# Sums, scores and outputs of a token block's four batches as one step each on TensorE, in a scan with a gated MLP behind it

## The chip, the cores and the metric

The kernel runs on one core of one Trainium2 chip. The metric is the device time of one execution in microseconds (us). The core's engines are called here as the profile calls them: PE (TensorE matmul) with PEld (its weight loads), DVE (VectorE), ACT (ScalarE), POOL (GpSimd, nearly idle here) and SP (SyncE, which issues most of the DMAs). Each engine works through its own instructions in the order in which they were issued to it; between engines they wait on semaphores.

## The reference

A chunked linear scan ("attention"), then a gated MLP on its output, all in float32. Cut to what is computed:

```python
# batch 4, heads H 8, sequence S 768, head size D 32, state size N 16
cum = cumsum(log(clip(a, 1e-6, 1)))             # within a chunk
M   = (C @ B^T) * exp(cum_i - cum_j) * causal   # "scores", times decays
y   = M @ x + (C @ state) * exp(cum)            # "outputs": own chunk + carried state
state = decay_full * state + sum_j B_j x_j * decay_from_j   # "sums"
# then, with all 8 heads side by side as 256 columns:
out = (silu(y @ w_gate) * (y @ w_val)) @ w_out  # d_model 256, d_ff 1536
```

## The kernel before

**Tiling.** The sequence is cut into NB = 6 token blocks of P = 128 positions, each block into K = 2 pieces of Q = 64. A block holds all four batches, so the MLP sees T = 4 x 128 = 512 columns per block. The hidden size is cut into NF = 12 slices f of 128.

**The scan part of block k.** `load_bc`, `load_aj`, `load_an` and `load_xb` fetch its data (tiles `bc`, `L`, `E`, `xb`). DVE turns the factors into decays with running scans (`scan_j` per batch on `L`, `scan_n` on `E`), weighs B with them (`weigh_b`, in `xb`, one instruction per batch) and C (`weigh_c`, in `bc`). PE then does three things, each per batch b, in small float32 matmuls: `sums` (tiles `st`: 8 matmuls per batch, what a piece adds to the state; 4 in the last block), `scores` (tiles `S`: 8 per batch) and the outputs (tiles `y`: `values`, 16 per batch, from `L` and `xb`, and `carried`, 8 per batch, from `bc` and the state `T`). In between, `apart` (ACT or DVE) takes `st` out of PSUM into `T`, `step` (DVE, `tmp` and `T`) carries the state on, and `mix` (DVE, `L<-S`) multiplies the scores with the decays. `st`, `S` and `y` of blocks 1 to 5 share a pool of four PSUM banks (`at`); `st` takes two of them, `S` and `y` all four. So `S` can't be written in full before `apart` is done, nor `y` before `mix` is.

**The MLP part of block k.** For every f, `gate_val` makes two products (tiles `gv` f 0 and f 1, "halves" below: in block 0 two float32 matmuls each, from block 1 on six fp32r matmuls each, with high and low parts of weights and of `y`, which are `xh` and `xl`). ACT takes the silu, DVE the product (both `sg`), then `hid_high` and `hid_low` split it (`hh`, `hl`; only HB = 4 buffers each), and `project` adds it up (tiles `po`, six matmuls per f). During block 0 and 1 the weights are also fetched and split, `wg` for the gates and `wo` for the projection: per weight tile a row of ACT and DVE instructions (`w_magnitude` to `w_low`), with one work buffer `w` for all `wo` tiles.

**What sets the order.** Every step is handed to a planner (`Plan`) with an engine or a choice of two, a cost, a rank, what it needs and which buffers it takes. The planner runs an estimate of all engines forward and issues steps by rank as they come ready; PE steps of another `kind` (`"f"` for the scan part, `"r"` for the MLP) get a small penalty at a change of kind. What comes out is a fixed order on each engine. So a change of one step's cost or size may also move steps on the other engines, and may move steps between ACT and DVE. Before the change, sums, scores and each batch's `values` and `carried` are a planner step of their own per batch (in block 0 `values` is one step per half of the heads), so MLP steps may come between two batches. All instructions go through one helper, so each has line 192 in the profile, and tiles tell them apart.

Of the kernel before, what the change touches and what calls it, by code (L numbers as in the profile page):

```python
# [17 lines left out]
BATCH, H, S, D, N = 4, 8, 768, 32, 16  # L18
# [6 lines left out]
T = BATCH * P  # L25
NB = S // P
W = Q + 1
NP = H // 2
# [14 lines left out]
class Plan:  # L43
# [19 lines left out]
    def add(self, engine, cost, run, rank, needs=(), takes=(), uses=(), gives=None, kind=None, lag=0.0, rows=1.0, slack=0.0):  # L63
        engines = [(engine, cost)] if cost is not None else engine
        self.ops.append(Op(engines, run, rank, needs, takes, uses, gives, kind, lag, rows, slack))
# [137 lines left out]
def scan_moe_kernel(ctx: ExitStack, tc, aj, an, bc, xb, wgv, wo, cst, sel, out):  # L203
# [34 lines left out]
    def piece(q):  # L238
        return slice(Q * q, Q * q + Q)
# [129 lines left out]
    def banks(k, name, n):  # L369

        where, tag = (ps_mm, "mm") if k == 0 and name in ("S", "y") else (ps_at, "at")
        return [where.tile([P, 512], F32, tag=tag, name=f"{name}{k}_{i}") for i in range(n)]

    def pair(p):
        return slice(2 * N * p, 2 * N * p + 2 * N)

    def scores(k, b):

        c = bl[k]
        if not b:  # L380
            c["S"] = [
                t.rearrange("p (b h i) -> p b h i", h=2, i=Q) for t in banks(k, "S", NP)
            ]
        for q in range(K):
            for p in range(NP):
                te.matmul(
                    c["S"][p][piece(q), b], c["B"][pair(p), b, piece(q)],
                    c["Cz"][pair(p), b, :, piece(q)], start=True, stop=True,
                )
# [6 lines left out]
    def last(k, q):  # L396
        return k == NB - 1 and q == K - 1

    def sums(k, b):

        c = bl[k]
        if not b:
            c["st"] = [
                t[:, : BATCH * 2 * D].rearrange("p (b c) -> p b c", c=2 * D)
                for t in banks(k, "st", K - last(k, K - 1))
            ]
        for p in range(NP):
            for q in range(K - last(k, K - 1)):
                te.matmul(
                    c["st"][q][pair(p), b], c["Bj"][piece(q), b, pair(p)],  # L410
                    c["x"][piece(q), b, 2 * D * p : 2 * D * p + 2 * D], start=True, stop=True,
                )
# [15 lines left out]
    def state(k, q):  # L428

        if q:  # L430
            return bl[k]["T"][:, q - 1]
        return bl[k - 1]["T"][:, K - 1] if k else None
# [10 lines left out]
    def values(k, bs, gs):  # L443

        c = bl[k]
        if not bs[0]:
            t = banks(k, "y", K * len(gs))
            for q in range(K):
                for g in gs:
                    c["y"][2 * q + g] = t.pop(0)[:, : BATCH * Q].rearrange("p (b i) -> p b i", i=Q)  # L450
        L = c["L"].rearrange("p (b h) t -> p b h t", h=H)
        for b in bs:
            for h in range(4 * gs[0], 4 * gs[-1] + 4):
                for q in range(K):
                    o = D * (h % 4)
                    te.matmul(
                        c["y"][2 * q + h // 4][o : o + D, b], c["x"][piece(q), b, D * h : D * h + D],
                        L[piece(q), b, h, :Q], start=b == 0, stop=state(k, q) is None,
                        skip_group_check=True,
                    )  # L460

    def carried(k, b):

        c = bl[k]
        for q in range(K):
            if state(k, q) is None:
                continue
            for p in (0, 2, 1, 3):
                o = 2 * D * (p % 2)
                te.matmul(  # L470
                    c["y"][2 * q + p // 2][o : o + 2 * D, b], state(k, q)[pair(p), b],
                    c["C"][pair(p), b, piece(q)], start=False, stop=True, skip_group_check=True,
                )

    xh, xl = {}, {}

# [175 lines left out]
    def do(f, *a):  # L652
        return lambda *e: f(*a, *e)
# [6 lines left out]
    add = plan.add  # L660
# [22 lines left out]
    for n, ranks in enumerate(IDLE):  # L683
        for i, r in enumerate(ranks):
            need = [("idle", n, i - 1)] if i else [("M", 0, 0)] if n else []
            takes = [] if i else [("at", ("rest", n))]
# [24 lines left out]
    for k in range(NB):  # L711
        r = due(k)
        SLACK = min(k / 2, 1.0)
        z = -5 if not k else r + LEAD[min(k, 3)]
        L, E, BC, XB, CZ, TT = ("L", k), ("E", k), ("bc", k), ("xb", k), ("Cz", k), ("T", k)
# [3 lines left out]
        def behind(key):  # L719
            return [(key, k - 1)] if k else []  # L720

        q = ("SP", 0.48) if k else ("-", 0.0)
# [6 lines left out]
        if not k:  # L729
# [4 lines left out]
            for b in range(BATCH):  # L734
                r = z + 0.5 + b
                for i in range(2 if b < SPREAD else 0):
                    t = ("spread", b, i)
                    add("PE", 0.45, do(spread, b, i), r + 0.5 * i, ["clip", "pick"], takes=[("at", t)], uses=[t, "rows"], gives=t, kind="s", rows=0.1)
                    need = [t, ("decays", 0), "dj"] + ([("scan0", b)] if i else [])
# [16 lines left out]
        st = [("st", k, q) for q in range(K - last(k, K - 1))]  # L756
        S = [("S", k, p) for p in range(NP)]
        y = [("y", k, i) for i in range(2 * K)]
        for b in range(BATCH):
            add("PE", 0.3, do(sums, k, b), z + 3 + 1.4 * b if k else -1.5, [("bt", k, b), *([("st", k, b - 1)] if b else [])], takes=[] if b else [("at", i) for i in st], uses=st, gives=("st", k, b), kind="f", rows=1.0, slack=SLACK)  # L760
            add("PE", 0.35, do(scores, k, b), z + 3.5 + 1.4 * b if k else -1.9 + 0.1 * b, ([("Cz", k), ("st", k, BATCH - 1)] if k else [("Cz", k)]) + ([("S", k, b - 1)] if b else []), takes=[] if b else [("at" if k else "mm", i) for i in S], uses=[*S, CZ], gives=("S", k, b), kind="f", rows=1.0, slack=SLACK)
        done = [("S", k, b) for b in range(BATCH)]
        add("-", 0.0, do(new_states, k), z + 2, behind("T"), takes=[("T", TT)], gives=("T", k))
        for q in range(len(st)):
            add([("Act", 0.65), ("DVE", 0.36)], None, do(apart, k, q), z + 4 + 0.5 * q, [("st", k, b) for b in range(BATCH)] + [("T", k)], uses=[st[q]], gives=("ap", k, q))
        for p in range(NP):
            add("DVE", 0.6, do(mix, k, p), z + 8 + 0.5 * p if k else (-1.25, -1.24, -1.1, -1.1)[p], [*done, *(("L", k, b) for b in range(BATCH))], uses=[S[p]], gives=("M", k, p))
        before = [("step", k - 1, K - 1)] if k else []
        for q in range(0 if k else 1, len(st)):
            need = [*before, ("E", k), ("ap", k, q)] + ([] if k or q > 1 else [("ap", k, 0)])  # L770
            add("DVE", 0.75, do(step, k, q), z + (8 if k else 25) + q, need, takes=[("tmp", ("tmp", k, q))], uses=[("tmp", k, q)] + ([("T", k - 1)] if k and not q else []), gives=("step", k, q))
            before = [("step", k, q)]
        uses = [L, E, XB, BC, *y, TT]
        steps = [("step", k, q) for q in range(len(st))] if k else [("ap", 0, 0)]
        if k:
            uses.append(("T", k - 1))
        for g in range(0 if k else 2):
            need = [("M", 0, p) for p in (2 * g, 2 * g + 1)]
            add("PE", 0.8, do(values, 0, range(BATCH), (g,)), -1.4 + 0.1 * g, need, takes=[("mm", y[2 * q + g]) for q in range(K)], uses=[L, XB, *y], gives=("vals", g), kind="f")
        for b in range(BATCH):  # L780
            if k:
                add("PE", 0.35, do(values, k, (b,), (0, 1)), z + 11 + 1.4 * b, [("M", k, p) for p in range(NP)] + ([("val", k, b - 1)] if b else []), takes=[] if b else [("at", i) for i in y], uses=[L, XB, *y], gives=("val", k, b), kind="f", rows=1.0, slack=SLACK)
            else:
                add("-", 0.0, lambda: None, z, [("vals", 0), ("vals", 1)], gives=("val", 0, b))
            add("PE", 0.5, do(carried, k, b), z + 11.7 + 1.4 * b if k else -1, [("val", k, b), ("ce", k), *steps], uses=uses, gives=("y", k, b), kind="f", rows=1.0, slack=SLACK)
        done = [("y", k, b) for b in range(BATCH)]
        if not k:
            add("-", 0.0, new_whole, -9, ["clip"], takes=[("x", "xf")], gives="xf")
            for i in range(2 * K):
# [8 lines left out]
    for k in range(NB):  # L798
        xs = [(t, k, i) for t in ("xh", "xl") for i in range(2 * K)]
        for f in range(NF):  # L800
            r = due(k, f)
            need = [*xs, ("wh", f), ("wl", f)]
            c = 1.4
            if not k:
                need = [("round", f), *(("xf", i) for i in range(2 * K))]
# [12 lines left out]
        for n, (m, t, fs) in enumerate(sums_of(k)):  # L818
            b = ("po", k, m, t)
            need = [x for f in fs for x in (("hl", k, f), ("wh", NF + f // 2), ("wl", NF + f // 2))]  # L820
# [73 lines left out]
```

## Time and profile before

| | |
|---|---|
| median of 3 runs | 368.54 us (368.12 to 368.83) |
| the profiled execution: its time, its span | 370.03 us, 368.3 us |
| PE busy | 358.2 us, 97% of the span, granted clock 1.000 |
| PEld / DVE / ACT busy | 273.1 / 232.5 / 125.2 us |
| DMA | 28.62 MB, 78 GB/s mean |

The span runs from the first to the last instruction; 1.73 us of the profiled execution lie outside it. "Busy" is the share of time in which at least one instruction ran. A busy PE is not a PE at its peak, since matmuls overlap. Stages in time, by the matmuls on PE: block 0's scan part up to 22 us, block 0's gates with block 1's scan part up to 74 us, block 1's gates up to 107 us, the projections of blocks 0 and 1 with block 2's scan part up to 150 us, then for block 2, 3 and 4 gates (with the scan part of the next block) and projection, 55 us each, then block 5's gates and projection.

### The profile page before, as it was taken

Reading aid. Unit: us, or ns where it says so; the run is one execution under the profiler, and the core shown is the slowest. Engines: PE = TensorE matmul, PEld = TensorE weight load, DVE = VectorE, ACT = ScalarE, POOL = GpSimd, SP = SyncE. Lnnn points to the kernel's source line nnn. Section 1 sums busy time; section 2 is a strip of 40 time slices with the busy share of each in tenths; the row PEclk is TensorE's granted clock in tenths of the full one; section 3 lists DMA queues with packets and bytes.
Section 4 is the critical chain, followed back from the end, with each engine's and each line's share of the span. In section 5 each row is a group of like instructions: output and inputs, shape, how many; then the busy total and the mean of one; then the engine's idle time right before and its main releaser. Section 6 shows DMA issues by size and latency. Waiting matters only on the chain.

```text
span 368.3 us, 7584 instructions
## 1 busy us (share of the span) xinstructions
PE 358.2 (97%) x3293; PEld 273.1 (74%) x3293; DVE 232.5 (63%) x412; ACT 125.2 (34%) x221; POOL 0.8 (0%) x6
## 2 busy tenths in 40 slices
PE   8989999999999989999999999999999999999996
PEld 6855345478877867887788887788887788888895
DVE  3998899999998659255348655349554344352241
ACT  3453773533342443222243221243221233221242
POOL 0000000000000000000000000000000000000000
PEclk9999999999999999999999999999999999999999
DMA  7659732781100760100083100082100000100001
GB/s 223 239 175 241 230 125 73 230 217 58 59 0 4 183 162 0 59 0 3 4 205 83 60 0 2 4 211 78 57 1 2 4 0 2 57 0 2 0 0 59
DMA packets 8737, 28.62 MB, mean 78 GB/s; under 512 B 1008, under 2 KB 1912, under 8 KB 8064
## 3 DMA queue, kind: packets, MB, share of 16 engines
q1 hardware_dynamic: 8416, 26.82, 25.2%
q10 hardware_dynamic: 288, 1.31, 1.0%
q8 instruction: 26, 0.43, 0.5%
q14 instruction: 7, 0.06, 0.1%
HBM read 24.79 MB, written 3.35 MB: 76 GB/s over the span
## 4 chain that ended last, share of the span: by engine, by line
PE 73%; DVE 13%; DMA 9%; issue 2%; ACT 1%; SPq 1%; DVEq 0%; ACTq 0%
PE gv L192 43%; PE po L192 22%; PE y L192 4%; DMA xb<-in_xb 4%; DMA wg5r<-in_wgv 4%; DVE L L192 3%; DMA L<-in_aj 2%; PE S L192 2%; DVE sg L192 2%; PE rest L192 1%; PE st L192 1%; SPq L192 1%; DVE wo3w L192 1%; DVE xb L192 1%; DVE wo4w L192 1%
## 5 line engine op out<-in xcount | busy, mean ns | idle before, releaser
L192 DVE TENSOR_TENSOR sg<-gv,sg 128x512 f32<-128x512 f32 x72 | 49.5, 688 | 85.9 <-PE gv L192 81.5
L192 ACT ACTIVATE sg<-gv 128x512 f32<-128x512 f32 x72 | 42.7, 594 | 102.8 <-PE gv L192 102.8
L192 DVE TENSOR_TENSOR hl<-sg,hh 128x512 fp32r<-128x512 f32 x72 | 48.9, 686 | 18.2 <-ACT hh L192 17.7
L192 ACT CAST hh<-sg 128x512 fp32r<-128x512 f32 x55 | 34.2, 622 | 50.1 <-PE po L192 35.9
L192 DVE TENSOR_TENSOR_SCAN L<-L,dj 128x520 f32<-128x520 f32 x21 | 25.8, 1232 | 5.1 <-DMA L<-clipped 5.1
L192 DVE TENSOR_TENSOR L<-S,L 128x512 f32<-128x512 f32 x24 | 15.1, 683 | 1.6 <-PE S L192 1.6
L192 PEld LDWEIGHTS <-unit 128*128 128x128 bf16 x141 | 11.1, 119 | 4.9 <-issue 3.7
L192 ACT COPY ob<-po 128x512 f32<-128x512 f32 (+1 forms) x13 | 7.2, 555 | 21.1 <-PE po L192 20.6
L192 PE MATMUL rest<-unit 128*128 128x128 bf16 x141 | 12.5, 258 | 1.1 <-DVE warm L192 1.1
L192 PE MATMUL y<-bc,T 32*64 32x64 f32 x352 | 10.2, 229 | 1.3 <-issue 1.3
L192 PE MATMUL po<-hl,wo1h 128*128 128x512 f32 (+1 forms) x26 | 9.9, 382 | 1.2 <-DVE hl L192 1.2
L192 PE MATMUL y<-L,xb 64*32 64x64 f32 x768 | 10.9, 222 | 0.0
L192 PEld LDWEIGHTS y<-L,xb 64*32 64x32 f32 x768 | 7.4, 105 | 4.0 <-issue 2.2
L192 ACT ACTIVATE Cz<-bc,cs 128x512 f32<-128x512 f32 x10 | 6.7, 716 | 10.7 <-DMA bc<-in_bc 7.6
L192 PE MATMUL po<-hl,wo2h 128*128 128x512 f32 (+1 forms) x26 | 9.9, 382 | 0.3 <-DVE hl L192 0.3
L192 PEld LDWEIGHTS y<-bc,T 32*64 32x64 f32 x352 | 7.1, 131 | 4.2 <-issue 2.5
L192 PE MATMUL po<-hh,wo0h 128*128 128x512 f32 (+1 forms) x26 | 9.9, 382 | 0.0
L192 PEld LDWEIGHTS S<-Cz,bc 32*64 32x64 f32 x384 | 6.8, 144 | 4.2 <-issue 2.9
L192 PE MATMUL po<-hh,wo2h 128*128 128x512 f32 (+1 forms) x26 | 9.8, 378 | 0.0
L192 PE MATMUL po<-hh,wo1h 128*128 128x512 f32 (+1 forms) x26 | 9.7, 374 | 0.0
L192 PE MATMUL po<-hl,wo0h 128*128 128x512 f32 (+1 forms) x26 | 9.7, 374 | 0.0
L192 PE MATMUL po<-hl,wo4h 128*128 128x512 f32 (+1 forms) x26 | 9.7, 374 | 0.0
(285 smaller groups left out, 792.2 us busy)
## 6 DMA issues: line engine op xcount, KB each, us to landing
L<-clipped SPq DMA_DIRECT2D x10, 520.0 KB
xb<-in_xb SPq DMA_DIRECT2D x5, 768.0 KB, 11.8
out<-ob SPq DMA_DIRECT2D x11, 256.0 KB, 2.1
bc<-in_bc SPq DMA_DIRECT2D x5, 512.0 KB
E<-clipped SPq DMA_DIRECT2D x5, 260.0 KB
xb<-in_xb ACTq DMA_DIRECT2D x1, 768.0 KB, 5.5
bc<-in_bc ACTq DMA_DIRECT2D x1, 512.0 KB
wg0r<-in_wgv SPq DMA_DIRECT2D x1, 512.0 KB
```

The lines of the kernel that those rows point to most:

```text
L192: ins = getattr(self.engine, name)(*a, **k)
```

## The change

From block 1 on, the four batches of `sums` are one planner step, the four of `scores` another, and `values` and `carried` of all batches a third (`outputs`). Nothing can be placed inside a step. The instructions themselves, their sizes and their order inside a step stay; only the steps that the planner orders have changed, with their costs (0.8, 1.2 and 3.2 in place of 0.3, 0.35 and 0.35 + 0.5 per batch) and what they wait for: `sums` now needs all four batches' weighed B (`bt`) before it starts, `outputs` needs `mix`, `weigh_c` and the state before its first matmul. In block 0 the steps stay as they were, but a zero-cost step ahead of each `carried` is gone.

```diff
-    def scores(k, b):
+    def scores(k, bs):
+        for b in bs:
+            scores_of(k, b)
+
+    def scores_of(k, b):
 ...
-    def sums(k, b):
+    def sums(k, bs):
+        for b in bs:
+            sums_of_pieces(k, b)
 ...
+    def outputs(k):
+        for b in range(BATCH):
+            values(k, (b,), (0, 1))
+            carried(k, b)
 ...
-        for b in range(BATCH):
-            add("PE", 0.3, do(sums, k, b), z + 3 + 1.4 * b if k else -1.5, [("bt", k, b), *([("st", k, b - 1)] if b else [])], ...)
-            add("PE", 0.35, do(scores, k, b), z + 3.5 + 1.4 * b if k else -1.9 + 0.1 * b, ...)
-        done = [("S", k, b) for b in range(BATCH)]
+        for bs in [(b,) for b in range(BATCH)] if not k else [range(BATCH)]:
+            b, more = bs[-1], bs[0]
+            n = len(bs)
+            add("PE", 0.3 if n == 1 else 0.8, do(sums, k, bs), -1.5 if not k else z + 3, [*(("bt", k, i) for i in bs), ...], ...)
+            add("PE", 0.35 if n == 1 else 1.2, do(scores, k, bs), z + 3.5 if k else -1.9 + 0.1 * b, ...)
+        done = [("S", k, BATCH - 1)]
 ...
-        for b in range(BATCH):
-            if k:
-                add("PE", 0.35, do(values, k, (b,), (0, 1)), z + 11 + 1.4 * b, [("M", k, p) for p in range(NP)] + ([("val", k, b - 1)] if b else []), ...)
-            else:
-                add("-", 0.0, lambda: None, z, [("vals", 0), ("vals", 1)], gives=("val", 0, b))
-            add("PE", 0.5, do(carried, k, b), z + 11.7 + 1.4 * b if k else -1, [("val", k, b), ("ce", k), *steps], ...)
-        done = [("y", k, b) for b in range(BATCH)]
+        if k:
+            need = [*(("M", k, p) for p in range(NP)), ("ce", k), *steps]
+            add("PE", 3.2, do(outputs, k), z + 11, need, takes=[("at", i) for i in y], ...)
+        for b in range(0 if k else BATCH):
+            add("PE", 0.5, do(carried, 0, b), -1, [("vals", 0), ("vals", 1), ("ce", 0), *steps], ...)
+        done = [("y", k)]
```

**How it moves instructions.** In block 2 the order on PE stays as it was: sums, scores and outputs had each come out as one piece before. In blocks 1 and 3 to 5 they had not. In block 3 (and likewise in 4 and 5) before, PE did half of the sums, gate slice 6, the other half, half a slice of gates, the scores, three halves, the outputs up to the third batch's `values`, gate slice 9, and the rest of the outputs; in block 1 the sums were split by gate slice 6 and the outputs by gate slice 9.

PE in block 3, around the end of the first half of the sums; numbers at the end of names count buffers. Before:

```order
L192 MATMUL st_1_1831<-xb_1512 32x64
L192 MATMUL gv_6_0_1849<-xh_979,wg6h 128x512 x2
L192 MATMUL gv_6_0_1849<-xh_979,wg6l 128x512 x2
L192 MATMUL gv_6_0_1849<-xl_980,wg6h 128x512 x2
L192 MATMUL gv_6_1_1856<-xh_979,wg6h 128x512 x2
L192 MATMUL gv_6_1_1856<-xh_979,wg6l 128x512 x2
L192 MATMUL gv_6_1_1856<-xl_980,wg6h 128x512 x2
L192 MATMUL st_0_1830<-xb_1512 32x64
```

PE in block 3, around the end of all of the sums. After:

```order
L192 MATMUL st_1_1831<-xb_1512 32x64
L192 MATMUL gv_6_0_1865<-xh_978,wg6h 128x512 x2
L192 MATMUL gv_6_0_1865<-xh_978,wg6l 128x512 x2
L192 MATMUL gv_6_0_1865<-xl_979,wg6h 128x512 x2
L192 MATMUL S_0_1878<-Cz_1527,bc_1487 64x128
L192 MATMUL S_1_1879<-Cz_1527,bc_1487 64x128
L192 MATMUL S_2_1880<-Cz_1527,bc_1487 64x128
L192 MATMUL S_3_1881<-Cz_1527,bc_1487 64x128
```

The sums are no longer resumed behind slice 6; the scores follow half a slice after the sums in both versions, and now five halves, not three, lie between scores and outputs.

DVE at the end of block 1's gates, where block 2's sums are taken out of PSUM (`T<-st`) between the last weight tiles' steps. Before:

```order
L192 TENSOR_TENSOR sg_10_1222<-gv_10_1_1215,sg_10_1222 128x512
L192 TENSOR_SCALAR wo5w<-wo5w 128x512 x2
L192 SCALAR_TENSOR_TENSOR wo5w<-wo5r,wo5w 128x512
L192 TENSOR_TENSOR sg_11_1246<-gv_11_1_1239,sg_11_1246 128x512
L192 ISA wo5w<-wo5r,wo5w 128x1024
L192 TENSOR_TENSOR T_928<-st_1_1252,cs 128x256
```

DVE at the same place. After:

```order
L192 TENSOR_TENSOR wo4l<-wo4w,wo4h 128x512
L192 TENSOR_TENSOR sg_11_1240<-gv_11_1_1232,sg_11_1240 128x512
L192 TENSOR_TENSOR T_900<-st_0_1246,cs 128x256
L192 TENSOR_SCALAR wo5w<-wo5w 128x512
L192 TENSOR_TENSOR tmp_0_1297<-T_106,E_899 128x256
```

`T<-st` now stands ahead of the steps of weight tile `wo5`, of which four stood ahead of it. (`ISA` is `CUSTOM_DVE_ANT_0` in the profile.)

DVE during block 2's projection, where block 4's decays (`L`) and weighed B (`xb`) are made between the low parts `hl` that the projection waits for. Before:

```order
L192 TENSOR_TENSOR hl_6_2171<-sg_6_1863,hh_6_2170 128x512
L192 SCALAR_TENSOR_TENSOR L_2093<-L_2093,dj 128x520
L192 TENSOR_TENSOR hl_7_2182<-sg_7_1907,hh_7_2181 128x512
L192 TENSOR_TENSOR xb_2114<-xb_2114,L_2093 128x128
L192 TENSOR_TENSOR hl_8_2192<-sg_8_1962,hh_8_2191 128x512
```

DVE at the same place. After:

```order
L192 TENSOR_TENSOR xb_2097<-xb_2097,L_2076 128x128 x2
L192 TENSOR_TENSOR hl_6_2173<-sg_6_1914,hh_6_2172 128x512
L192 SCALAR_TENSOR_TENSOR L_2076<-L_2076,dj 128x520
L192 TENSOR_TENSOR hl_7_2185<-sg_7_1945,hh_7_2184 128x512
L192 TENSOR_TENSOR xb_2097<-xb_2097,L_2076 128x128
L192 SCALAR_TENSOR_TENSOR L_2076<-L_2076,dj 128x520
L192 TENSOR_TENSOR hl_8_2196<-sg_8_1962,hh_8_2195 128x512
```

The first two `xb` steps, which need the `xb` load, moved from behind `hl_7` to ahead of `hl_6`, and one more scan (`SCALAR_TENSOR_TENSOR` on `L`) stands ahead of `hl_8`. On SP the order of the DMAs is the same but for one pair: block 1's `E` load now goes ahead of weight tile `wg5r`'s, not behind it.

More of the change, by code (lines that the diff above doesn't have):

```diff
@@ L397, in last, with sums_of_pieces @@
         return k == NB - 1 and q == K - 1
-    def sums(k, b):
+    def sums(k, bs):
+        for b in bs:
+            sums_of_pieces(k, b)
+    def sums_of_pieces(k, b):
         c = bl[k]
@@ L758, in scan_moe_kernel @@
         y = [("y", k, i) for i in range(2 * K)]
-        for b in range(BATCH):
-            add("PE", 0.3, do(sums, k, b), z + 3 + 1.4 * b if k else -1.5, [("bt", k, b), *([("st", k, b - 1)] if b else [])], takes=[] if b else [("at", i) for i in st], uses=st, gives=("st", k, b), kind="f", rows=1.0, slack=SLACK)
-            add("PE", 0.35, do(scores, k, b), z + 3.5 + 1.4 * b if k else -1.9 + 0.1 * b, ([("Cz", k), ("st", k, BATCH - 1)] if k else [("Cz", k)]) + ([("S", k, b - 1)] if b else []), takes=[] if b else [("at" if k else "mm", i) for i in S], uses=[*S, CZ], gives=("S", k, b), kind="f", rows=1.0, slack=SLACK)
-        done = [("S", k, b) for b in range(BATCH)]
+        for bs in [(b,) for b in range(BATCH)] if not k else [range(BATCH)]:
+            b, more = bs[-1], bs[0]
+            n = len(bs)
+            add("PE", 0.3 if n == 1 else 0.8, do(sums, k, bs), -1.5 if not k else z + 3, [*(("bt", k, i) for i in bs), *([("st", k, more - 1)] if more else [])], takes=[] if more else [("at", i) for i in st], uses=st, gives=("st", k, b), kind="f", slack=SLACK)
+            add("PE", 0.35 if n == 1 else 1.2, do(scores, k, bs), z + 3.5 if k else -1.9 + 0.1 * b, ([("Cz", k), ("st", k, BATCH - 1)] if k else [("Cz", k)]) + ([("S", k, more - 1)] if more else []), takes=[] if more else [("at" if k else "mm", i) for i in S], uses=[*S, CZ], gives=("S", k, b), kind="f", slack=SLACK)
+        done = [("S", k, BATCH - 1)]
         add("-", 0.0, do(new_states, k), z + 2, behind("T"), takes=[("T", TT)], gives=("T", k))
         for q in range(len(st)):
-            add([("Act", 0.65), ("DVE", 0.36)], None, do(apart, k, q), z + 4 + 0.5 * q, [("st", k, b) for b in range(BATCH)] + [("T", k)], uses=[st[q]], gives=("ap", k, q))
+            add([("Act", 0.65), ("DVE", 0.36)], None, do(apart, k, q), z + 4 + 0.5 * q, [("st", k, BATCH - 1), ("T", k)], uses=[st[q]], gives=("ap", k, q))
         for p in range(NP):
@@ L779, in scan_moe_kernel @@
             add("PE", 0.8, do(values, 0, range(BATCH), (g,)), -1.4 + 0.1 * g, need, takes=[("mm", y[2 * q + g]) for q in range(K)], uses=[L, XB, *y], gives=("vals", g), kind="f")
-        for b in range(BATCH):
-            if k:
-                add("PE", 0.35, do(values, k, (b,), (0, 1)), z + 11 + 1.4 * b, [("M", k, p) for p in range(NP)] + ([("val", k, b - 1)] if b else []), takes=[] if b else [("at", i) for i in y], uses=[L, XB, *y], gives=("val", k, b), kind="f", rows=1.0, slack=SLACK)
-            else:
-                add("-", 0.0, lambda: None, z, [("vals", 0), ("vals", 1)], gives=("val", 0, b))
-            add("PE", 0.5, do(carried, k, b), z + 11.7 + 1.4 * b if k else -1, [("val", k, b), ("ce", k), *steps], uses=uses, gives=("y", k, b), kind="f", rows=1.0, slack=SLACK)
-        done = [("y", k, b) for b in range(BATCH)]
+        if k:
+            need = [*(("M", k, p) for p in range(NP)), ("ce", k), *steps]
+            add("PE", 3.2, do(outputs, k), z + 11, need, takes=[("at", i) for i in y], uses=[L, *uses], gives=("y", k), kind="f", slack=SLACK)
+        for b in range(0 if k else BATCH):
+            add("PE", 0.5, do(carried, 0, b), -1, [("vals", 0), ("vals", 1), ("ce", 0), *steps], uses=uses, gives=("y", 0) if b == BATCH - 1 else ("y", 0, b), kind="f")
+        done = [("y", k)]
         if not k:
```

## The prediction

> **What bounds the kernel now.** I read the page first, then the busy time by stage, then the chain of waits, then the timelines at the places where the order on PE or DVE changes.
>
> ```profile
> span 368.3 us, 7584 instructions
> ...
> PE 358.2 (97%) x3293; PEld 273.1 (74%) x3293; DVE 232.5 (63%) x412; ACT 125.2 (34%) x221; POOL 0.8 (0%) x6
> ```
>
> PE is busy for 97%, so at most some 10 us of waits can go; the rest has to come out of what PE does. By stage (start and end, length, then each engine's busy time):
>
> ```profile
> 76.00:107.00 31.00, 31.00 (x138) 25.66 (x137) 30.09 (x52) 11.54 (x20) 0.00 (x0) 1.00 0.27 83
> 107.00:150.00 43.00, 40.29 (x467) 31.05 (x466) 31.80 (x57) 15.78 (x28) 0.00 (x0) 1.00 0.29 75
> 150.00:189.00 39.00, 39.00 (x466) 30.83 (x466) 18.42 (x34) 10.34 (x20) 0.00 (x0) 1.00 0.13 41
> ```
>
> Up to 107 us DVE (30.09 of 31.00) is as full as PE; from 107 to 150 PE loses 2.7 us; from 150 on PE is the bound without a gap, and DVE has room. So an edit of PE's order can pay in full behind 150 us, and before that only where DVE lets it.
>
> **Term 1: islands of small matmuls in blocks 3 to 5.** The chain of waits (start, length, work) through block 2's gates, which hold block 3's scan part:
>
> ```profile
> 150.21 16.32 PE gv L192 x72
> 166.53 0.39 PE st L192 x32
> 166.92 2.94 PE gv L192 x12
> 169.86 0.39 PE st L192 x32
> 170.25 1.58 PE gv L192 x6
> 171.83 1.14 PE S L192 x63
> 172.96 4.31 PE gv L192 x18
> 177.27 1.94 PE y L192 x128
> 179.21 2.94 PE gv L192 x12
> 182.15 1.17 PE y L192 x64
> 183.32 5.68 PE gv L192 x24
> 189.00 16.34 PE po L192 x72
> ```
>
> Undisturbed, 72 gate matmuls take 16.32 us: 0.227 each, 1.36 per half slice, 2.72 per slice. A slice between two islands takes 2.94, a half 1.58, three halves 4.31 against 4.08, four halves 5.68 against 5.44: every stretch behind an island costs 0.22 to 0.24 more, whatever its length. That is the price of leaving the gates and coming back, and it is all that an island costs beside its own matmuls. Before, five islands (sums, sums, scores, outputs, outputs); now three: the split of sums and that of outputs go. Working it out anew: 16.32 + sums 0.78 + half 1.58 + scores 1.14 + five halves 4.31 + 2.72 + outputs 1.94 + 1.17 + three slices 5.68 + 2.72 = 38.36 us, against 38.79 from 150.21 to 189.00. So 0.43 us per block, 0.22 per island. Blocks 4 and 5 have the same order and islands: 3 x 0.43 = **-1.3 us**. The sums, scores and outputs keep their number of matmuls. No new wait should arise on PE: block 3's weighed B is due a whole stage earlier (DVE is busy for only 18.42 of the 39 us), between sums and scores there is still one half (1.58 us) in which the four sums banks' worth of `T` is taken out, as before, and the way from scores to outputs grows by two halves.
>
> The Trainium skill (TensorEngine Tiling, Key Properties) says that a change of tiling mode drains TensorE, and TensorE: Matmul & The Clock Gate, Single matmul latency, puts the fixed part of a lone warm matmul at 398 cycles of 2.4 GHz. As an estimate from that page, two full drains of 0.17 us for each of six islands would be 2.0 us in place of 1.3. The rows show 0.22 per island, not 0.33, so part of the drain must be covered, and I keep the rows.
>
> **Term 2: the wait ahead of block 2's scores.** PE's order there does not change, DVE's does. PE's timeline (start, length, instruction, idle time before it):
>
> ```profile
> 107.41 0.86 PE L192 MATMUL st<-xb 64*32 64x64 f32 x64
> 108.20 0.50 PE L192 MATMUL po<-hh,wo0h 128*128 128x512 f32 x1
> ...
> 109.80 0.43 PE L192 MATMUL S<-Cz,bc 32*64 32x128 f32 x4
> 111.35 1.17 PE L192 MATMUL S<-Cz,bc 32*64 32x128 f32 x60 [1.12 <-DVE T L192]
> 112.46 0.50 PE L192 MATMUL po<-hh,wo0h 128*128 128x512 f32 x1
> ```
>
> ```profile
> 110.28 0.68 DVE L192 CUSTOM_DVE_ANT_0 wo5w<-wo5r,wo5w 128x1024 uint16<-128x1024 uint16 x1
> 110.88 0.42 DVE L192 TENSOR_TENSOR T<-st,cs 128x256 f32<-128x256 f32 x1
> 111.22 0.42 DVE L192 CAST wo5h<-wo5w 128x512 fp32r<-128x512 f32 x1
> ```
>
> The sums are done at 108.2, but DVE takes its half of them out only at 110.88, behind the work on weight tile `wo5`. In the new order `T` stands ahead of all of that. DVE's steps follow each other by 0.60 (the long ones, 110.28 to 110.88) or 0.34 (the short ones, 110.88 to 111.22). By the two DVE orders, what is done before this `T` loses four `wo5` steps (two long, two short), four casts and one scaling (short) to ACT or to later, and gains four short ones: 1.2 + 7 x 0.34 = 3.6 us less and 1.4 more, 2.2 us net. So DVE could be there at 108.7, right behind the sums. The scores then start at 109.80 and run through: 1.14 us by the chain's row, so the projection resumes at 110.94, not at 112.46: **-1.5 us**. Bounds: nothing, if DVE is as late as before; 1.5 if `T` ends before 109.80, for which DVE has 0.75 us to spare (108.7 + 0.34 against 109.80). I take the upper end, since 2.2 us less work is nearer to it than none. ACT takes the other half in both versions. What is late next: `mix` must end before the outputs, now 4.3 us behind the scores as before; with the `T` steps and one `hl` ahead of it, it has over a microsecond left. `wo5`'s steps move behind, and the projection first needs them at its eleventh slice, 10 us later. The outputs' end releases block 3's loads (SP waits for it), so the loads, and what waits for them later in that stage, come as much earlier and stay as long.
>
> **Term 3: block 1's part, up to 52 us.** PE's timeline, where block 0's gates hold block 1's sums:
>
> ```profile
> 43.66 3.67 PE L192 MATMUL gv<-xf,wg5w 128*128 128x512 f32 x8 [0.75 <-ACT hh L192]
> 47.26 0.34 PE L192 MATMUL st<-xb 64*32 64x64 f32 x16
> ...
> 52.08 0.35 PE L192 MATMUL st<-xb 64*32 64x64 f32 x16 [0.46 <-DVE xb L192]
> ```
>
> From 43.66 to the sums' end at 52.4 PE needs two slices, the sums, 0.46 of waiting for the fourth batch's weighed B and one island's price. In the new order all sums stand behind slice 6, where three quarters of them stood, and ahead of that B DVE has two casts and a scaling less and a copy more (0.7 us less); I expect no wait, 0.46 less, and 0 to 0.22 for the island, and the like for the outputs' split at slice 9. Against it stands the start: slice 5 waits for weight tile `wg5`, whose DMA is now issued behind `E`:
>
> ```profile
> 25.86 0.53 SPq L192 DMA_DIRECT2D wg5r<-in_wgv  x1
> 26.48 0.62 SPq L192 DMA_DIRECT2D E<-clipped  x1
> ```
>
> and DVE now does two more scans of `L` ahead of `wg5`'s steps, one of which used to stand between them and one behind. The issue alone is 0.6 us later; slice 5 may start anywhere from no later to 0.9 later; I take 0.4. Together 0.46 + 0.3 - 0.4, about **-0.4 us**, between -0.9 and +0.4.
>
> **Term 4: `xb` and scans ahead of `hl`.** During block 2's and 3's projection the outputs, now ended before slice 9, release the next block's loads one slice earlier, but DVE's queue has the first `xb` steps ahead of `hl_6`, and a scan more ahead of `hl_8`. DVE before, and SP's issue of that load:
>
> ```profile
> 198.26 0.29 DVE L192 TENSOR_TENSOR xb<-xb,L 128x128 f32<-128x128 f32 x1 [0.33 <-DMA xb<-in_xb]
> 198.47 0.68 DVE L192 TENSOR_TENSOR hl<-sg,hh 128x512 fp32r<-128x512 f32 x1
> 199.07 0.28 DVE L192 TENSOR_TENSOR xb<-xb,L 128x128 f32<-128x128 f32 x1
> 199.27 1.23 DVE L192 TENSOR_TENSOR_SCAN L<-L,dj 128x520 f32<-128x520 f32 x1
> 200.42 0.67 DVE L192 TENSOR_TENSOR hl<-sg,hh 128x512 fp32r<-128x512 f32 x1
> ```
>
> ```profile
> 186.57 0.62 SPq L192 DMA_DIRECT2D xb<-in_xb  x1
> ```
>
> The load lands 11.7 us after its issue. Issued 2.94 earlier (one slice), it lands at 195.3. Then come two `xb` (0.2 each), `hl_6` 0.6, a scan 1.15, `hl_7` 0.6, `xb` 0.2, a scan 1.15 and `hl_8` 0.6: 200.0. PE, its projection starting at 189.00 - 0.43 + 0.2 by where the outputs begin, wants `hl_8` at its second matmul of the ninth slice: 188.8 + 8 x 1.36 + 0.23 = 199.9. So it is a tenth late or a few tenths early, in two projections. I take **+0.3 us** in all, between 0 and +1.
>
> **Sum.** -1.3 - 1.5 - 0.4 + 0.3 = -2.9 us. The profiled execution took 370.03 us (1.73 of it outside the span), so it would be 367.1; the runs' median lies 1.5 lower at 368.54, which gives **365.7 us**.
>
> **Rivals.** *The scores' wait stays.* If DVE reaches `T` as late as before, or ACT does, term 2 is gone: 365.7 + 1.5 = 367.2. For it speaks that DVE was 97% busy from 76 to 107 and its chain through the `wo` tiles is serial, with one buffer; against it that `wo5` no longer stands in front. The skill's TensorEngine Tiling, PSUM Bottleneck, warns that PSUM's evacuation may become the bound when small matmuls are packed; this wait is such a case.
>
> *Nothing measurable.* Terms 2 and 3 both fail and the early stage loses as much again as term 1 brings: `wg5` late by 1 us or more and DVE's backlog carried into block 1's gates, which wait for free banks: -1.3 + 0.3 + 1 = 368.5. The trace has PE waiting only 0.75 us there, so this needs several tenths in more than one place.
>
> *Slower.* The `xb` load lands late and blocks `hl_6` and all behind it. Block 3's load, in the chain, took longer:
>
> ```profile
> 122.34 13.57 DMA xb<-in_xb
> ```
>
> With 13.57 in place of 11.7 it lands at 197.2, and `hl_8` comes at 201.9, 2 us late, in both projections: +4 in place of +0.3, 365.7 + 3.7 = 369.4. It turns the gain into a loss from a landing some 13.2 us after the issue. Against it: block 4's load took 11.7 with the same neighbours in the queue.
>
> **How the numbers follow.** Forecast 0.63, the scores' wait 0.17, nothing 0.11, slower 0.09. 0.2% of the time, about what a measurement of this kernel can tell from no change, is 0.74 us: faster means below 367.8, slower above 369.3. The first two are faster; of the last a third would land within the bound because only one projection is hit. Faster 0.80, same 0.14, slower 0.06. The forecast's own bounds: term 1 fixed, term 3 from -0.9, term 4 from 0, gives 364.9, and 0.3 for the runs' own spread 364.6; upwards the range takes in the scores' wait and half of a late load, 367.9.
>
> **What would show it.** Right: three islands per block in the chain from 150 us on and 38.4 us from the first gate of block 2 to its projection; no wait of the scores for `T` near 110 us, and the projection resuming 1.1 to 1.2 us after the scores begin; sums of block 1 in one piece without a wait for `xb`; PE idle below 8 us in all. Wrong: `po <- DVE hl` waits in block 2's or 3's projection beyond 0.5 us each, slice 5 of block 0 waiting over 1.6 us, `S <- T` waits in any block.

## The result, and the profile after

The changed kernel takes 371.67 us (median of 20 executions, 369.48 to 375.07) against 368.80 us for the kernel before (20 executions): ratio 1.0069, 95% interval 1.0045 to 1.0094. It is slower, by some 2.5 us, where 2.9 us less was forecast. The profiled execution took 372.27 us with a span of 370.5. The ratios here and below leave out executions that were disturbed, so they and not the medians are what is compared.

The page of the changed kernel, span and busy time of the engines:

```profile
span 370.5 us, 7585 instructions
...
PE 358.0 (97%) x3293; PEld 275.0 (74%) x3293; DVE 231.6 (63%) x410; ACT 127.2 (34%) x223; POOL 0.8 (0%) x6
```

PE does the same 3293 matmuls in the same busy time (358.2 before). What grew is its waiting. PE's waits (what it waited for, us in total, times, longest), of after and then the two rows of before that belong beside them:

```profile
PE y L192 <- issue: 5.3, 4, 1.6
PE gv L192 <- ACT wg7w L192: 1.5, 1, 1.5
...
PE po L192 <- DVE hl L192: 0.6, 2, 0.3
```

```profile
PE po L192 <- DVE hl L192: 1.5, 3, 0.8
PE y L192 <- issue: 1.3, 1, 1.3
```

The first row is new in size: four times PE stops inside the outputs (`y`) for nothing that the profile shows ("issue"), once in block 0 as before, and now once in each of blocks 3, 4 and 5. The chain of waits through block 3's gates, which hold block 4's scan part, shows one:

```profile
203.62 16.32 PE gv L192 x72
219.94 0.79 PE st L192 x53
220.73 1.60 PE gv L192 x6
222.33 1.14 PE S L192 x63
223.47 7.04 PE gv L192 x30
230.51 2.58 PE y L192 x146
233.09 1.21 issue
234.30 0.84 PE y L192 x39
235.13 8.40 PE gv L192 x36
```

Three islands, as the order said, and the two stretches of gates behind them cost what was forecast (1.60 and 7.04). But the outputs take 230.51 to 235.13, 4.62 us, where block 1's, with the same 192 matmuls in one piece, take 3.10:

```profile
60.55 3.10 PE y L192 x192
```

Taken from the same views, the clock at the start of each stage (first gate of the block):

```
                    before    after    difference, and of the stage alone
block 2's gates     150.21    146.82   -3.4   -3.4
block 3's gates     205.34    203.62   -1.7   +1.7
block 4's gates     260.45    259.86   -0.6   +1.1
block 5's gates     315.50    317.74   +2.2   +2.8
end                 368.3     370.5    +2.2    0.0
```

So the early stages brought 3.4 us, more than forecast, and the three stages with stalled outputs lost 5.6. Block 5's outputs, in the last of these, are followed by something else. PE's timeline there, and the busy time by stretch (length, busy time of PE, PEld, DVE, ACT, POOL, then the granted clock):

```profile
288.81 0.32 PE L192 MATMUL y<-L,xb 64*32 64x64 f32 x9
290.57 0.42 PE L192 MATMUL y<-L,xb 64*32 64x64 f32 x23 [1.44 <-issue]
290.93 0.46 PE L192 MATMUL y<-bc,T 32*64 32x64 f32 x16
291.32 0.73 PE L192 MATMUL gv<-xh,wg9h 128*128 128x512 f32 x2
```

```profile
288.50:292.00 3.50, 2.06 (x67) 1.58 (x68) 0.64 (x2) 0.65 (x2) 0.00 (x0) 1.00 0.02 5
292.00:295.50 3.50, 3.50 (x10) 2.70 (x9) 1.44 (x5) 0.60 (x1) 0.00 (x0) 0.52 0.00 0
```

For 3.4 us behind that stall the granted clock is 0.52, and the 36 gate matmuls behind the outputs take 10.03 us by the chain where those behind block 4's outputs take 8.40: another 1.6 us.

### The profile page after: what moved, and what is told of

Read it like the earlier page. It is cut to its first block, busy times and chain, and to the rows that moved or that the text cites. A ratio compares the mean times of both kernels' runs of the same rounds, so it can differ in the third digit from the quotient of the medians.

```text
span 370.5 us, 7585 instructions
## 1 busy us (share of the span) xinstructions
PE 358.0 (97%) x3293; PEld 275.0 (74%) x3293; DVE 231.6 (63%) x410; ACT 127.2 (34%) x223; POOL 0.8 (0%) x6
## 4 chain that ended last, share of the span: by engine, by line
PE 67%; DMA 14%; DVE 12%; issue 3%; ACT 2%; SPq 1%; DVEq 0%; ACTq 0%
PE gv L192 40%; PE po L192 17%; PE y L192 4%; DMA wg6r<-in_wgv 4%; DVE L L192 3%; DMA bc<-in_bc 3%; DMA xb<-in_xb 3%; DMA L<-clipped 2%; DVE hl L192 2%; PE rest L192 2%; PE a L192 1%; PE S L192 1%; DVE sg L192 1%; PE st L192 1%; DMA wo4r<-in_wo 1%
## 5 line engine op out<-in xcount | busy, mean ns | idle before, releaser
L192 PE MATMUL y<-L,xb 64*32 64x64 f32 x768 | 11.7, 223 | 3.8 <-issue 3.8
L192 DVE CAST xh<-y 128x256 fp32r<-128x256 f32 x9 | 3.4, 417 | 11.5 <-PE y L192 11.5
L192 PE MATMUL po<-hl,wo3h 128*128 128x512 f32 (+1 forms) x26 | 9.8, 378 | 0.0
L192 ACT CAST xh<-y 128x256 fp32r<-128x256 f32 x11 | 3.5, 377 | 18.2 <-PE y L192 18.2
L192 PE MATMUL po<-hh,wo2l 128*128 128x512 f32 (+1 forms) x26 | 9.7, 374 | 0.0
```

The source lines that it names most:

```text
L192: ins = getattr(self.engine, name)(*a, **k)
```

## What an issue wait is here

Counting every record of PE in order of time (matmuls, weight loads, its few instructions that only wait), the first record behind the waits in `y` of after has the numbers 706, 3778, 4802 and 5826. Divided by 256 each leaves 194 (before's one wait, in block 0, stands at 706 as well). So all stand at a border of blocks of 256 instructions. The same holds for every issue wait of PE in the twelve traces of this case: 21 waits, all with the rest 194. The trace also has a DMA queue for instructions:

```profile
q8 instruction: 26, 0.43, 0.5%
```

26 packets of 16,384 bytes, which is 64 bytes for each of 256 instructions; and PE's 6626 records hold 26 borders with that rest, at the numbers 194, 450 and so on up to 6594. Theory A, then: PE's instructions come in blocks of 256. Each matmul of an island stands with its weight load for two instructions and takes 16 ns (3.10 us for 192), so a block that lies wholly inside the outputs (384 instructions) is used up in 2.1 us, and the next block is not there. In gates a block lasts 29 us. The Trainium skill (Runtime: NRT & Kernel Launch, Instruction fetch mechanics) says the same of the blocks, 16 KiB or 256 instructions, fetched while the one before is executed, and calls the cost of crossing a border mostly hidden. The trace agrees with the blocks; hidden the crossing is only where a block lasts long enough.

Theory A makes the stall hang on where a border falls, not on what is done. The rivals: B, a long row of small matmuls stalls PE by its length, wherever it stands; C, the loss is in the merged sums and scores, the new load times or the clock, and the issue waits only go along.

## The experiments

### Block 3's sums issued twice (the changed kernel with more work)

```
     def sums(k, bs):
         for b in bs:
             sums_of_pieces(k, b)
+        for b in bs if k == 3 else ():
+            sums_of_pieces(k, b, True)      # same banks, same values once more
```

> The changed kernel with block 3's sums issued twice in a row (the second pass writes the same values again): 32 matmuls of the program more on PE, 128 records with their weight loads, and no other instruction moved on any engine. Theory A (PE runs out of instructions: its stream comes in blocks of 256 instructions, weight loads counted, and a block that lies wholly inside the outputs is used up in 2.1 us, faster than the next one comes, 3.3 to 3.9 us; so the loss hangs on where the blocks' borders fall): the added 128 move the borders out of blocks 3, 4 and 5; no issue wait in their outputs, which take 3.1 us each in place of 4.4 to 4.8; sums of block 3 longer by 0.65 to 0.8 us; time 371.7 - 4.6 + 0.7 = 367.8 us, 366.3 to 368.5. Rival B (a long row of small matmuls stalls PE by its length, wherever it stands): the three waits of 1.1 to 1.4 us stay, 372.4. Rival C (the time is lost to the granted clock and to late loads, and the issue waits only go along): 372.4 as well.

Measured: 367.10 us, ratio to before 0.9919 (0.9884 to 0.9953). More work, and some 5.5 us less than the changed kernel by the two ratios (1.5% of 369). The chain through block 3's gates, with block 4's scan part:

```profile
201.80 16.32 PE gv L192 x72
218.12 0.79 PE st L192 x53
218.91 1.59 PE gv L192 x6
220.50 1.14 PE S L192 x61
221.63 7.03 PE gv L192 x30
228.67 3.07 PE y L192 x182
```

The outputs take 3.07 us, and no issue wait is left but block 0's. From the gates' first to the projection's first matmul (201.64 to 240.01 in PE's timeline) it is now 38.37 us, the forecast's 38.36. B and C, which expected 372.4, fall. Of the 5.5 us A accounts for 3.9. The clock, at half here from 7.24 us on for 10.24 us, does not drop behind a stall in any later stage, which can make up part of the rest. The mean granted clock of each execution, which is on record, agrees without proving it: read in stretches of 3.4 us at half clock, 13 of the 19 executions of the changed kernel that are compared have one or four of them (in this trace the start alone takes three), and 1 of 11 here. Where such a stretch stood, a mean does not tell.

### Block 1's sums issued twice

The same edit with `k == 1`: the same added work, the borders moved by the same 128 instructions, but from block 1 on.

> The same added work, but block 1's sums are issued twice in place of block 3's. By theory A the borders move by 128 instructions from block 1 on: they leave blocks 3, 4 and 5 as in the kernel with block 3's sums twice, and now one block of instructions lies wholly inside the outputs of block 1 and one inside those of block 2. So issue waits of 1.1 to 1.4 us in the outputs of blocks 1 and 2, none in 3 to 5; 371.7 - 4.6 + 0.7 + 2 x 1.4 = 370.6 us, or 369.2 if block 2's stall is hidden behind the wait for its xb load. Rival B: three waits in blocks 3 to 5 and none in 1 and 2, 372.4. Rival C: 372.4, or less if block 1 hides the added work.

Measured: 369.05 us, ratio 0.9982 (0.9949 to 1.0014). The stalls are gone from blocks 3 to 5 and stand in blocks 1 and 2. PE's timeline in these two:

```profile
61.80 0.32 PE L192 MATMUL y<-L,xb 64*32 64x64 f32 x9
62.89 0.42 PE L192 MATMUL y<-L,xb 64*32 64x64 f32 x23 [0.77 <-issue]
...
118.31 0.30 PE L192 MATMUL y<-L,xb 64*32 64x64 f32 x5
118.84 0.44 PE L192 MATMUL y<-L,xb 64*32 64x64 f32 x27 [0.23 <-issue]
```

A said where: a border stands 307 instructions into block 1's outputs, and the wait comes behind 153 matmuls (144 and 9) with their weight loads, 306 records. The waits are smaller than the 1.4 us expected, and the time is accordingly nearer to the lower of A's two figures.

### Outputs alone split again, and outputs alone merged

First, the changed kernel with before's output steps; second, the kernel before with the new one:

```
-            add("PE", 3.2, do(outputs, k), z + 11, ...)
+            add("PE", 0.35, do(values, k, (b,), (0, 1)), z + 11 + 1.4 * b, ...)
+            add("PE", 0.5, do(carried, k, b), z + 11.7 + 1.4 * b, ...)
```

> The changed kernel with the outputs alone put back to steps of one batch, so that in blocks 3 to 5 (and 1) slice 9 stands again between two and a half batches and the rest; sums and scores stay in one piece. Theory A: no block of 256 instructions lies wholly inside a row of small matmuls, no issue wait beyond block 0; one island more in blocks 1, 3, 4 and 5 (0.22 us each): 371.7 - 4.6 + 0.9 = 368.0 us, 367.2 to 368.6. Rival B expects the same 368.0 (shorter rows). Rival C (merged sums, scores and the loads' new times are what costs): 371.7 + 0.2.

> The kernel before with the outputs alone made one step; sums and scores stay in steps of one batch as before. Theory A: issue waits in the outputs of blocks 3, 4 and 5, which take 4.4 to 4.8 us in place of 3.1; one island less in blocks 1, 3, 4 and 5: 368.8 - 0.9 + 4.6 = 372.5 us, 371.0 to 373.0. Rival B: the same. Rival C (sums, scores or the loads are to blame): 368.8 - 0.9 = 367.9.

Measured: split again 369.67 us, ratio 1.0008 (0.9978 to 1.0038); outputs alone merged 370.62 us, ratio 1.0052 (1.0013 to 1.0091). So most of the slowing comes with the outputs, against C, as far as these two tell: with the outputs' steps the planner moved instructions on DVE and ACT too. And the two miss their figures by 1.7 and 1.9 us, one above and one below. Why, of the first, from PE's waits with outputs split again:

```profile
PE st L192 <- DVE xb L192: 2.9, 1, 2.9
PE y L192 <- issue: 1.8, 1, 1.8
...
PE S L192 <- DVE T L192: 1.0, 1, 1.0
```

The only issue wait is block 0's, as expected. But block 2's scores wait for `T` again, as before the change, though `T` has kept its new place in DVE's order, ahead of `wo5`'s steps:

```profile
111.87 0.41 DVE L192 TENSOR_TENSOR T<-st,cs 128x256 f32<-128x256 f32 x1
112.20 0.42 DVE L192 TENSOR_SCALAR wo5w<-wo5w 128x512 f32<-128x512 f32 x1
```

DVE comes to it at 111.87 us, 2.6 later than in the changed kernel (109.29), while PE's scores begin only 1.2 later (110.89 for 109.69). So the place in the order alone does not save the wait; DVE must also arrive in time. How much of its lateness is this execution's own start (the 2.9 us stand at 13 us) and how much the moved steps, one trace does not tell, and of the 1.7 us it explains 1.0. In the second, the stalls are not all there. PE's timeline in blocks 3 and 4 of the outputs alone merged:

```profile
179.06 0.45 PE L192 MATMUL y<-L,xb 64*32 64x64 f32 x31
180.69 0.21 PE L192 MATMUL y<-L,xb 64*32 64x64 f32 x1 [1.18 <-issue]
180.84 0.46 PE L192 MATMUL y<-bc,T 32*64 32x64 f32 x16
181.23 1.04 PE L192 MATMUL gv<-xh,wg9h 128*128 128x512 f32 x2
...
236.91 0.58 PE L192 MATMUL y<-L,xb 64*32 64x64 f32 x32
```

Block 4's border is crossed without a wait. The instruction packets' own times say why (read from the trace's DMA records; all in us: when PE entered the block ahead of the border and how long it was in it, waits included, then when the packet started and landed and when PE went on behind the border):

```
kernel, block        entered, length  packet started   landed   PE goes on
after, 3             174.28, 3.27     174.92           176.10   177.56
after, 4             230.59, 3.71     231.70           232.83   234.30
after, 5             286.65, 3.93     287.66           289.10   290.57
sums 1 twice, 1       59.64, 3.24      60.51            61.44    62.89
sums 1 twice, 2      116.13, 2.71     116.46           117.41   118.84
outputs alone, 3     177.37, 3.33     178.06           179.33   180.69
outputs alone, 4     234.73, 2.32     234.74           235.69   237.05
outputs alone, 5     290.94, 3.12     291.69           292.82   294.06
```

At these eight borders PE goes on 1.24 to 1.47 us behind the landing; a packet takes 0.9 to 1.4 us; it starts 0.0 to 1.1 us after PE enters the block. Together 2.3 to 3.9 us for a block against 2.1 us of work in it, so a border inside the outputs costs from 0.05 to 1.7 us, as the packet happens to come. The clock dropped here too: the first gates behind block 3's outputs take 1.04 us, where the same row behind block 5's outputs in the changed kernel, still at the full clock, shows 0.73.

### Control: the kernel before with block 3's sums twice

```
     def sums(k, b):
         sums_of_pieces(k, b)
+        if k == 3:
+            sums_of_pieces(k, b, True)
```

> Control of what the repeated sums do by themselves: the kernel before with each of block 3's sums issued twice (the same values written again), 32 matmuls of the program more on PE. Before has slice 9 inside the outputs of blocks 3 to 5, so no block of 256 instructions lies wholly in them, with or without the shift. Theory A: the added work alone, +0.65 us to 0.8: 369.0 + 0.7 = 369.7 us. Rival D (the repetition helps by something else, such as the clock or later loads): some 4 us less, as it was in the changed kernel: 365.

Measured: 370.94 us, ratio 1.0024 (0.9987 to 1.0061), by the ratio 0.9 us more. (The trace is of an execution of 703.9 us, and no time is read from it.) The repetition by itself helps nothing; D falls.

### Smaller shifts: 64 and 32 instructions

The first experiment with only two batches repeated (`bs[:2]`), later with only one.

> The changed kernel with block 3's sums of the first two batches issued twice: half the shift, 64 instructions. Theory A, from where the borders then fall: in block 3 a border stands 32 instructions behind the outputs' start and the next one 288, so the block between lies wholly inside: an issue wait of 0.2 to 1.7 us there; in block 4 only one border (at 235 of 386) and in block 5 one at 245, with 11 to 21 instructions of gates ahead in the block that ends there (1.2 us and more): no wait in block 4, none or up to 0.4 in block 5. Time 367.1 - 0.3 + 1.4 = 368.2 us. Rival B (length): three waits. Rival D (the repetition helps in some other way): no wait in block 3 either, 366.8.

Measured: 367.90 us, ratio 0.9954 (0.9911 to 0.9998). The time fits, but by luck, since the place does not: block 3's outputs have no wait. From the chain of its one trace (an execution of 371.5 us):

```profile
178.01 3.08 PE y L192 x182
```

The packet for that border started at 176.70, 1.3 us before the outputs. In gates and projections, packets mostly start when PE has some 20 to 40 records to go to the border, so the instructions are read that far ahead; a border 32 instructions into the outputs is passed by the reader while the gates still run. A shift of 32 tests it:

> The changed kernel with only the first batch of block 3's sums issued twice: 32 instructions more. The borders then stand 64 and 320 instructions behind the start of block 3's outputs, 11 and 267 in block 4's, 21 and 277 in block 5's: a block lies wholly inside the outputs of each. Theory A as first put (every block wholly inside stalls): waits of 0.2 to 1.7 us in blocks 3, 4 and 5, 371.7 + 0.2 = 371.9 us. Theory A with reading ahead (the next block is asked for when PE is still some 40 instructions ahead of the border, as the records of slow stretches have it; a border under 40 instructions into the outputs is then reached while the gates still run): a wait in block 3 alone, none over 0.4 in blocks 4 and 5, 367.1 - 0.5 + 1.4 = 368.0 us, 367.2 to 369. Rival B: three waits, 371.9.

Measured: 367.48 us, ratio 0.9932 (0.9895 to 0.9969). PE's timeline in block 3, where the border stands at 64 and 320, and in block 4, where it stands at 11 and 267:

```profile
175.54 0.34 PE L192 MATMUL y<-L,xb 64*32 64x64 f32 x15
177.06 0.35 PE L192 MATMUL y<-L,xb 64*32 64x64 f32 x17 [1.19 <-issue]
...
232.04 0.45 PE L192 MATMUL y<-L,xb 64*32 64x64 f32 x32
```

One wait, in block 3, behind 159 matmuls (318 instructions), none in blocks 4 and 5: theory A with reading ahead, and not as first put. After's own waits had their first border 96, 43 and 53 instructions in by the same count, all beyond that reach, the second narrowly.

### A version without the stalls, at no added work

```
-        z = -5 if not k else r + LEAD[min(k, 3)]
+        z = -5 if not k else r + LEAD[k]
 ...
-IDLE = ..., [15.0 + 0.5 * i for i in range(24)]
-LEAD = {1: -30.0, 2: -44.0, 3: -44.0}
+IDLE = ..., [15.0 + 0.5 * i for i in range(15)]
+LEAD = {1: -30.0, 2: -44.0, 3: -44.0, 4: -52.2, 5: -52.2}
```

> The changed kernel with the borders moved by work that is left away or moved, not added: 9 of the 24 later pauses of block 0 (small matmuls whose result nobody reads, 54 instructions) are left out, and the scan parts of blocks 4 and 5 are due 8.2 us earlier, three slices. The borders then stand 232, 227, 151, 170 and 180 instructions behind the start of the outputs of blocks 1 to 5, one in each. Theory A: no issue wait from block 1 on; block 0's stays, its outputs' borders being where they were. Time: 367.1 without the repeated sums' 0.65 = 366.4 us, 365.4 to 367.5. Rival B: three waits, 371.7. What could spoil it: fewer pauses let PE idle in block 0, and the clock with it; then 367 to 368.

Measured: 366.19 us, ratio 0.9926 (0.9894 to 0.9958): as expected, and faster than both kernels. Since the edit also leaves out work and moves two scan parts, it shows the remedy and not, by itself, the cause. A second one takes the 9 pauses from the list ahead of block 0's outputs:

> As the kernel with the borders moved free, but the 9 pauses are taken from those ahead of block 0's outputs, so that their border, too, moves from 116 to 152 instructions behind the start of block 0's outputs (outputs of 416 instructions with the sums between). Theory A: no issue wait in any block, block 0's wait of 1.3 to 1.9 us at 20 us gone too. If that wait lies on the path: 366.4 - 1.4 = 365.0 us; since PE fills the time from there to 43 us with pauses until the gates' weights are ready, I expect most of it to be covered: 366.2. Rival: the clock falls with fewer pauses at the start: 367 to 368.

Measured: 365.00 us, ratio 0.9885 (0.9842 to 0.9927, 6 executions). That is the lower of the two figures above, but by luck: the wait whose end was to bring it is still there, and from 0.9926 the ratio is not told apart. PE's issue wait in the outputs, and blocks 2 to 4 by stage, in this version:

```profile
PE y L192 <- issue: 1.9, 1, 1.9
```

```profile
145.90:200.60 54.70, 54.70 (x537) 44.45 (x537) 31.27 (x53) 15.84 (x29) 0.00 (x0) 1.00 0.21 59
200.60:255.40 54.80, 54.80 (x538) 44.50 (x538) 30.98 (x52) 16.46 (x30) 0.00 (x0) 1.00 0.21 59
255.40:309.90 54.50, 54.50 (x506) 44.25 (x505) 23.12 (x39) 15.14 (x28) 0.00 (x0) 1.00 0.03 11
```

From block 2's gates on PE never waits, and each stage (145.95, 200.66, 255.38 and 309.88 are the gates' first matmuls) is 0.4 to 0.6 us under the kernel before's 55.1. Block 0's wait stayed, since its outputs with their sums are 416 instructions long and still held two borders. A third version moved these too (18 pauses left out ahead, 9 added behind):

> As the kernel in which block 0's border was moved too, mended: there block 0's outputs with their sums are 416 instructions long and still held the border at 408 of them, so the wait stayed (1.89 us). Now 18 pauses ahead of block 0's outputs are left out and 9 are added behind, so that only one border lies in block 0's outputs, 244 instructions in, and the block that ends behind them holds 45 instructions of pauses. Theory A: no issue wait over 0.5 us in any block. Time: if block 0's wait lies on the path, 365.0 - 1.5 = 363.5 us; if it is covered by the pauses until the gates' weights are ready, 365.0 as before. I expect it covered in part: 364.6, 363.3 to 366. Rival: without pauses at the start the clock is granted later: 366 and more.

Measured: 365.34 us, ratio 0.9861 (0.9808 to 0.9915, 6 executions), not told apart from 0.9885. PE's waits:

```profile
PE po L192 <- DVE hl L192: 2.1, 3, 0.9
PE y L192 <- DVE L L192: 2.0, 2, 1.8
...
PE st L192 <- issue: 0.2, 1, 0.2
```

The issue wait in `y` is gone and the gates begin at 21.39 us, 1.9 earlier than in the version before; but slice 5 starts at 42.54 us, where it started at 42.60. What PE gained there went into pauses and waits ahead of slice 5, so block 0's stall was covered.

## The prediction, step by step

**Term 1, the step that failed.** Its price of an island was right: without the stall, block 4's 4.62 us of outputs become 3.1 and 39.9 us from gates to projection become 38.4, as worked out, and the first experiment measured just that. What failed is the sentence "No new wait should arise on PE". It looked for a wait on data (`T`, the weighed B) and found none; the wait is for instructions. By the outputs' length against 3.10 us the three stalls cost 1.3, 1.5 and 1.7 us, together 4.6, and the clock's drop in block 5 another 1.6, against 1.3 gained; with 0.7 lost in block 2's projection (term 4) these are the 5.6 of the table. Slice 9, whose leaving was counted as 0.22 us saved, had been giving the next block of instructions 2.9 us to come. The trace of before had the sign in sight, the issue wait of 1.3 us in block 0's outputs, and the prediction did not read it.

**Term 2, right.** PE's scores of block 2, and DVE's `T`, in the changed kernel:

```profile
109.69 1.56 PE L192 MATMUL S<-Cz,bc 32*64 32x128 f32 x64
111.18 0.50 PE L192 MATMUL po<-hh,wo0h 128*128 128x512 f32 x1
```

```profile
109.29 0.41 DVE L192 TENSOR_TENSOR T<-st,cs 128x256 f32<-128x256 f32 x1
```

The scores run through and the projection resumes 1.5 us after they begin (1.1 to 1.2 was the sign named), at 111.18 in place of 112.46: 1.3 us, with 1.5 forecast. `T` came at 109.29, 0.6 later than reckoned, and still early enough. (The prediction speaks of four banks of sums there; they are two, and nothing hung on it.)

**Term 3, reached and then lost.** Block 1's sums run in one piece and do not wait for `xb`; slice 5 starts at 44.26, 0.6 late in place of 0.4, and its wait of 1.51 us lies just under the 1.6 named as a sign of failure. Block 1's gates begin at 73.58, where they began at 74.23, a little more than forecast; but they take 0.5 us longer, with a wait for ACT of 0.3 us at 82.60, and the first projection begins at 108.09 for 108.20. So 0.1 us of it was left: in small, what the rival of no measurable gain said of block 1's gates.

**Term 4, and a gain that was not reckoned.** In block 1's projection the load for block 3, issued 1.3 us earlier, also took less time:

```profile
121.00 11.48 DMA xb<-in_xb
```

Before, it took 13.57 us. The first weighing of `xb` stands ahead of `hl` on DVE and waits for the load in both kernels, up to 136.01 us before and 132.58 after; so `hl` now came earlier, and of the three waits for it, 1.5 us together, 0.3 is left. Block 1's projection takes 17.0 us in place of 19.1, and with what terms 2 and 3 had left by its start (1.2 and 0.1) this makes the 3.4 us of the early stages. I had carried the gain of term 2 on unchanged and looked for a loss only in blocks 2 and 3. Why the load took less time, no run here shows. In block 2's projection the loss came, 0.7 us (17.0 us in place of 16.3) for 0.3 in both; block 3's has none.

**The rivals.** None of them named the loss. The slower one (a late `xb` load) did not happen: the wait for `hl` in block 2's projection is 0.3, and block 3's has none. Of the signs, PE's idle time failed (12.5 us by the page, where below 8 was named) and told that something was wrong; the one that would have told what, an issue wait inside an island, was not listed.

## To carry to other kernels

Work between two rows of tiny matmuls may be what keeps PE in instructions: before joining such rows, count the instructions (weight loads too) and ask whether 256 of them in one piece last longer than the 2.3 to 3.9 us in which the next 256 came here. Whether a long row stalls hangs on where the borders fall, so an unrelated edit earlier in the program can bring or take away a microsecond per row; a few added or removed instructions move them. Read an "issue" wait by its place in the stream: if the record's number leaves the same rest by 256 each time, it is the supply.

## What the runs showed of the hardware that I had not expected

At the eight borders of the table PE goes on 1.24 to 1.47 us after the instruction packet of 16,384 bytes has landed. Where the block ahead of a border lies wholly inside the outputs of blocks 1 to 5, its packet starts from 2.6 us before to 1.1 us after PE enters that block; what sets the delay in between stays open. The granted clock fell to about half for 3.4 us behind two of the seven waits of 0.66 to 1.44 us that stood in the outputs of blocks 1 to 5 here (block 5 of after, block 3 of the outputs alone merged), and not behind the others. The Trainium skill (TensorE: Matmul & The Clock Gate, What's actually happening) has the clock fall to half after an idle window of 3413 ns. The drop's length agrees; a whole idle window it did not take, since PE was busy for 2.06 of the 3.5 us ahead of it. Why a wait of 1.18 us sufficed in one place and one of 1.21 did not in another, no run here shows.
